# Decode layer with adaLN, sliding-window attention and a GEGLU FFN: K and V loaded in pairs of tiles, all of K ahead of V, with fewer loads and a shorter list of filler matmuls

## The chip, the cores and the metric

The kernel runs on one core of one Trainium2 chip. The metric is the device time of one execution in microseconds (us). The core has a matrix engine (TensorE, PE in the profile; its weight loads are PEld), a vector engine (VectorE, DVE), a scalar engine (ScalarE, ACT), GpSimd (POOL) and SyncE (SP), which here issues the DMA transfers. Engines run side by side, each through its own list of instructions in order, and wait for one another by semaphores.

## What is computed

One decode step for two sequences (B = 2, one token each, D = 640): modulation vectors from `c`, a norm, attention of 32 heads of 192 over the last W = 1024 rows of the caches, an output projection, a second norm and a GEGLU FFN with F = 1536. All in bf16.

```python
mod = (silu(c) @ w_mod).reshape(B, 6, 1, -1)        # sa, ca, ga, sb, cb, gb
h = layernorm(x) * (1 + ca) + sa
q = (h @ wq).reshape(B, 1, 32, 192).transpose(0, 2, 1, 3)
k = k_cache[:, :, Sk - W:, :];  v = v_cache[:, :, Sk - W:, :]
p = softmax(einsum('bhqd,bhkd->bhqk', q, k) * 192 ** -0.5)
o = einsum('bhqk,bhkd->bhqd', p, v)
x = x + ga * (o.transpose(0, 2, 1, 3).reshape(B, 1, 32 * 192) @ wo)
h = layernorm(x) * (1 + cb) + sb
return x + gb * ((gelu(h @ w_gate) * (h @ w_up)) @ w_down)
```

## The kernel before

**Layout.** A partition holds one quarter of a head's window: 32 heads times 4 quarters are the 128 partitions, and each has KP = 256 rows of 192 values of K and as many of V, per sequence. These 256 rows are cut in NTL = 4 tiles of J = 64 rows, 24576 bytes per partition. So there are 8 tiles of K and 8 of V over the two sequences.

**The ring and the order of loads.** Tiles go through a ring of NS = 5 slots, `ring` (L178). `items` (L322 to L325) fixes their order: the four K tiles of sequence 0, then V of sequence 0 and K of sequence 1 in turns, then V of sequence 1. `declare_ring` (L332) issues, on SP, the load of the next tile as soon as the code has declared the use of the tile that held its slot; at run time SP then waits (at L93) until the last reader of that slot is done. SP's list in order: w_mod, wq in two loads, K tiles, the interleaved tiles, the four loads of wo (L585, into `r1`, where wq was), then w_gate, w_up in two and w_down in three loads (L589 to L601, into slots 1 and 2), and the store of the result (L663). Each is one instruction at L260.

**Stages.** w_mod's matmuls (L391) and the first norm give hT; q is two groups of matmuls as wq lands (L414); `qsel` (L433) spreads q to the partitions as `qbc`.

*K loop.* It works on half tiles. `d_mul` (L454) multiplies 32 rows of K with q on DVE, in place. `p_reduce` (L465) adds up twelve slices of 16 values each on TensorE, with the identity as weights, in a bank of PSUM, and `d_rows` (L474) adds up the remaining 16 values on DVE. `filler` puts ND = 4 matmuls whose result nobody reads (`warm`, L444) ahead of each `p_reduce`.

*Softmax* (L478 to L498) is done once per sequence: a maximum per head, by way of a transpose and a broadcast matmul, the exponential on ACT, and the sum.

*PV.* `d_mask` (L502) spreads the exponentials of a tile over the 32 heads on DVE, in one of two buffers `Em`; `p_pv` (L514) multiplies with V in 32 matmuls of 384 columns, two side by side, summed over all tiles in bank BK_O. PV of sequence 0 lies between the K steps of sequence 1; PV of sequence 1 stands alone, with eight fillers after each tile but the last.

*Rest.* `normalize` (L528 and L532), `p_sel` (L540) for both sequences, four copies to `oc`, three transposes to `oT` (L578), the wo matmuls (L609) in four groups, `x1`, the second norm (L355 to L378), gate and up (L628) with gelu on ACT, the product (L642), a transpose, the down matmuls (L651) in three groups, two vector steps (L659, L661) and the store. `warm` is called between these steps with the counts in WO_WARM and WD_WARM and those written at the calls. An `nc.Block` (L665) closes the program, with an exchange of events between all engines at its end.

**Waits.** `_track` (L42) derives the waits from names of buffers: a reader waits for the last writer, a writer for all readers; banks of PSUM count as written by whoever reads them.

Of the kernel before, what the change touches and what calls it, by code (L numbers as in the profile page):

```python
# [5 lines left out]
ALU = mybir.AluOpType  # L6
ACTF = mybir.ActivationFunctionType
AX = mybir.AxisListType
# [95 lines left out]
def bass_adaLN_cond__sliding_block_cached__geglu_ffn__decode_kernel(  # L104
# [34 lines left out]
    NTL = KP // J  # L139
    JH = J // 2  # L140
    NQ = H * Dh
# [4 lines left out]
    NQC = RN // QC  # L146
    SCALE = float(Dh) ** -0.5
# [6 lines left out]
    NS = 5  # L154
    SL = J * Dh
    WQ_SPLIT = [3, 2]
    assert sum(WQ_SPLIT) == KT
    WO_SPLIT = [16, 16, 12, 4]
    OT_SPLIT = [16, 16, 16]
    assert sum(WO_SPLIT) == NT and sum(OT_SPLIT) == NT  # L160
    WU_SPLIT = [3, 2]
    assert sum(WU_SPLIT) == KT
    WD_SPLIT = [6, 4, 2]
    assert sum(WD_SPLIT) == FT
    ND = 4

    WO_WARM = [2, 15, 2, 10]
    WD_WARM = [7, 2, 0]

    es = ExitStack()  # L170
    with es:
# [6 lines left out]
        ring = sb("ring", [P, NS, J, Dh], BF16)  # L178
        ring_f = ring[:, :, :, :].rearrange("p s j d -> p (s j d)")
        def slot_f(slot, a, n):  # L180
            assert a + n <= SL
            return ring_f[:, slot * SL + a:slot * SL + a + n]


        assert KT * 6 * D <= 2 * SL and 2 * KT * F + FT * D <= 2 * SL
        wm_f = ring_f[:, 2 * SL:2 * SL + KT * 6 * D]
        wm_v = wm_f.rearrange("p (k n) -> p k n", k=KT)
        Qsel = slot_f(4, 0, 2 * HM * P).rearrange("p (b m n) -> p b m n", b=2, m=HM)
        qC = slot_f(4, 2 * HM * P, RN)
        wg_v = ring_f[:, SL:SL + KT * F].rearrange("p (k n) -> p k n", k=KT)  # L190
        wu_v = ring_f[:, SL + KT * F:SL + 2 * KT * F].rearrange("p (k n) -> p k n", k=KT)
        wd_v = ring_f[:, SL + 2 * KT * F:SL + 2 * KT * F + FT * D].rearrange("p (f n) -> p f n", f=FT)
        oc = slot_f(4, 0, RN)
        oT = slot_f(4, RN, NT * SQ).rearrange("p (t m) -> p t m", m=SQ)
        aC = slot_f(3, 0, FN)
        aT = slot_f(3, FN, FT * SQ).rearrange("p (f m) -> p f m", m=SQ)
# [3 lines left out]
        one = sb("one", [1, 1], F32)  # L200
# [20 lines left out]
        Sg = sb("Sg", [P, max(KP, FN)], F32)  # L221
        S_sb = Sg[:, 0:KP]
        gl = Sg[:, 0:FN]
        ones_f = Sg[:, 0:P]
        M1 = sb("M1", [P, 1], F32)
        gm = sb("gm", [1, H], F32)
        gx = sb("gx", [1, H, QP], F32)
        nb = sb("nb", [P, 1], F32)
        E_sb = sb("E_sb", [P, KP], BF16)
# [7 lines left out]
        BK_O = 3  # L237
# [13 lines left out]
        sem_wq = [S.sem("d_wq%d" % i) for i in range(len(WQ_SPLIT))]  # L251
        sem_wo = [S.sem("d_wo%d" % i) for i in range(len(WO_SPLIT))]
        sem_wg = S.sem("d_wg")
        sem_wu = [S.sem("d_wu%d" % i) for i in range(len(WU_SPLIT))]
        sem_wd = [S.sem("d_wd%d" % i) for i in range(len(WD_SPLIT))]
        sem_ring = [S.sem("d_ring%d" % i) for i in range(NS)]
# [9 lines left out]
        def dram_rows(v):  # L266
# [7 lines left out]
        S.op("pool", lambda e: e.memset(one[:, :], 1.0), writes=["one"], name="one")  # L274
        S.op("pool", lambda e: e.memset(ones_f, 1.0), writes=[("S", 0, 0), ("S", 0, 1), ("S", 1, 0), ("S", 1, 1)], name="ones_f")
        S.op("pool", lambda e: e.affine_select(out=ident_f[:, :], in_=ones_f, pattern=[[-1, P]],
                                                compare_op=ALU.is_equal, fill=0.0, base=0, channel_multiplier=1),
             reads=[("S", 0, 0), ("S", 0, 1), ("S", 1, 0), ("S", 1, 1)], writes=["ident_f"], name="ident_f")
# [3 lines left out]
        S.op("pool", lambda e: e.memset(Qsel, 0.0), writes=[("ring", 4, 0)], name="Qsel0")  # L282
# [18 lines left out]
        for b in range(2):  # L301
            for m in range(HM):
                S.op("dve", (lambda b, m: lambda e: e.tensor_copy(
                    out=Qsel[:, b, m, :].rearrange("p (a m t) -> p a m t", a=NJ, m=HM)[:, :, m, :],
                    in_=ident_f[:, BS * b:P:SQ].unsqueeze(2).broadcast_to([P, NJ, QP])))(b, m),
                    reads=["ident_f"], writes=[("ring", 4, 0)], name="Qsel%d%d" % (b, m))

        def half_key(slot, hf):
            return ("ring", slot, hf)

        def ring_keys(slot):
            return [half_key(slot, 0), half_key(slot, 1)]

        keep = {}
        S.dma("sp", k_dma(wm_f, w_mod.rearrange("(p k) n -> p (k n)", k=KT)), sem_wm, writes=ring_keys(2) + ring_keys(3), name="ld_wm")
        wq_src = A_wq.rearrange("(p k) n -> p k n", k=KT)
        wq_of = [(sum(WQ_SPLIT[:i]), sum(WQ_SPLIT[:i + 1])) for i in range(len(WQ_SPLIT))]
        keep["wq_dma"] = [S.dma("sp", k_dma(wq_v[:, ka:kb, :].rearrange("p k n -> p (k n)"), wq_src[:, ka:kb, :].rearrange("p k n -> p (k n)")),
                                sem_wq[i], writes=[("wq", i)], name="ld_wq%d" % i) for i, (ka, kb) in enumerate(wq_of)]


        items = [("k", 0, t) for t in range(NTL)]  # L322
        for t in range(NTL):
            items += [("v", 0, t), ("k", 1, t)]
        items += [("v", 1, t) for t in range(NTL)]  # L325
        place = {it: n for n, it in enumerate(items)}
        ring_state = {"next": 0, "done": set()}

        def slot_of(*it):
            return place[it] % NS  # L330

        def declare_ring(*consumed, upto=len(items)):  # L332
            ring_state["done"].update(place[it] for it in consumed)
            while ring_state["next"] < upto and (ring_state["next"] < NS or (ring_state["next"] - NS) in ring_state["done"]):
                n = ring_state["next"]
                kind, b, t = items[n]
                slot = n % NS
                cache = A_v_cache if kind == "v" else A_k_cache
                S.dma("sp", k_dma(ring[:, slot, :, :].rearrange("p j d -> p (j d)"),
                                  cache[b, :, K0:Sk, :].rearrange("h (q r) d -> h q r d", q=QP)[:, :, J * t:J * (t + 1), :].rearrange("h q r d -> h q (r d)")),  # L340
                      sem_ring[slot], writes=ring_keys(slot), name="ld_%s%d_%d" % (kind, b, t))
                ring_state["next"] += 1

        declare_ring(upto=2)


# [37 lines left out]
        def mod_part(part):  # L384
# [10 lines left out]
            S.op("pe", f, reads=["scT"] + ring_keys(2) + ring_keys(3), writes=[bank(bk)], name="mod%d" % part)  # L395
# [9 lines left out]
        declare_ring(upto=4)  # L405


        for i, (ka, kb) in enumerate(wq_of):
            def f(e, ka=ka, kb=kb):
                last = None  # L410
                for k in range(ka, kb):
                    for c in range(NQC):
                        for j in range(NJ):
                            last = e.matmul(ps[SQ * j:SQ * j + SQ, BK_H + c, 0:QC], lhsT=hT[:, k, :],  # L414
                                            rhs=wq_v[:, k, RN * j + QC * c:RN * j + QC * (c + 1)],
                                            start=(k == 0), stop=(k == KT - 1), tile_position=(0, SQ * j), skip_group_check=True)
                return last
            keep["q"] = S.op("pe", f, reads=["hT", ("wq", i)], writes=[bank(BK_H + c) for c in range(NQC)], name="q%d" % i)

# [29 lines left out]
        def filler(n=1):  # L449
            warm(n * ND, BK_W)  # L450

# [264 lines left out]
```

## Time and profile before

| | |
|---|---|
| median of three runs | 189.1 us (189.08, 189.10, 189.87) |
| profiled execution: span from first to last instruction | 187.5 us |
| PE busy | 131.9 us, 1068 matmuls |
| DVE busy | 107.1 us, 114 instructions |
| ACT, POOL busy | 13.9 us, 4.9 us |
| HBM read | 76.88 MB, 410 GB/s over the span |
| loads of K, of V | 8 and 8, 3072 KB each |
| readerless matmuls (L444) | 174, 34.6 us |
| chain that ended last, by engine | DMA 53%, PE 21%, DVE 20% |

The median lies 1.6 us above the span of the profiled execution; the sums below are made against the span. A row of the profile names the line of the kernel, the engine, the operation, out<-in, the number of instructions and the busy time. The page's shares are averages over the whole span, so that each stage has to be looked at by itself, in the timeline and in windows. The granted clock is the share of its full speed that TensorE was allowed. The chain of waits is followed back from the last instruction, at each step to what released it.

### The profile page before, as it was taken

To read this page: it belongs to the slowest core of one execution; us is meant where nothing else is said; L and a number is where in the kernel's file an instruction comes from. 1 tells how busy PE (TensorE), PEld (TensorE's weight loads), DVE (VectorE), ACT (ScalarE), POOL (GpSimd) and SP (SyncE) were. 2 spreads that over 40 slices of the span, in tenths; PEclk is the share of its full clock that TensorE was granted. 3 is DMA by queue.
4 is the path that set the end of the run, shared out by engine and by line. 5 is a ranking of instruction groups with operands and counts; after the bars stand their busy time and mean duration, and the time that the engine had idled before them with its cause. 6 is when DMAs were issued, how large, how long until landed. Compare 5 with 4: busy or idle time off the path is not lost.

```text
span 187.5 us, 2388 instructions
## 1 busy us (share of the span) xinstructions
PE 131.9 (70%) x1068; PEld 65.3 (35%) x1068; DVE 107.1 (57%) x114; ACT 13.9 (7%) x24; POOL 4.9 (3%) x12
## 2 busy tenths in 40 slices
PE   0004543565999989449999939929539998859993
PEld 0001221251443333125454514504225656535441
DVE  6811400029599998389599398298475602903431
ACT  2003200031000000000000000000010002300400
POOL 8100000000000000000000000000000000000000
PEclk9999999555699999966999996987957999999999
DMA  7999899999999999999999999999999999999980
GB/s 262 394 457 440 385 454 412 425 451 440 435 425 421 419 418 440 451 430 430 425 419 412 430 456 435 428 419 425 419 435 446 427 424 424 421 412 420 414 345 5
DMA packets 4221, 77.02 MB, mean 411 GB/s; under 512 B 500, under 2 KB 500, under 8 KB 1140
## 3 DMA queue, kind: packets, MB, share of 16 engines
q1 hardware_dynamic: 4188, 76.88, 96.3%
q8 instruction: 8, 0.13, 0.3%
q10 hardware_dynamic: 24, 0.01, 0.0%
q14 instruction: 1, 0.01, 0.0%
HBM read 76.88 MB, written 0.00 MB: 410 GB/s over the span
## 4 chain that ended last, share of the span: by engine, by line
DMA 53%; PE 21%; DVE 20%; issue 2%; SPq 2%; ACT 0%; DVEq 0%
DMA ring<-in_A_k_cache_dram 31%; DMA r<-in_A_wo_dram 22%; DVE ring L454 14%; PE ps L465 8%; PE ps L444 5%; PE ps L514 4%; DVE Sg L474 2%; SPq L260 2%; PE ps L609 1%; DVE Em L502 1%; PE ps L628 1%; PE ps L651 1%; DVE ring L348 0%; ACT E_sb L493 0%; DVE ring L642 0%
## 5 line engine op out<-in xcount | busy, mean ns | idle before, releaser
L454 DVE TENSOR_TENSOR ring<-ring,qbc 128x6144 bf16<-128x6144 bf16 x16 | 53.5, 3352 | 10.6 <-DMA ring<-in_A_k_cache_dram 10.6
L465 PE MATMUL ps<-ring,ident_b 128*128 128x512 bf16 x192 | 50.0, 416 | 10.9 <-DVE ring L454 10.8
L444 PE MATMUL ps<-qbc,ident_b 128*128 128x384 bf16 x174 | 34.6, 333 | 2.9 <-issue 2.2
L465 PEld LDWEIGHTS ps<-ring,ident_b 128*128 128x128 bf16 x192 | 19.2, 104 | 38.5 <-DVE ring L454 15.0
L514 PE MATMUL ps<-ring,Em 128*64 128x384 bf16 x256 | 26.3, 367 | 4.9 <-DVE Em L502 4.9
L444 PEld LDWEIGHTS ps<-qbc,ident_b 128*128 128x128 bf16 x174 | 15.9, 100 | 18.5 <-issue 8.4
L514 PEld LDWEIGHTS ps<-ring,Em 128*64 128x64 bf16 x256 | 15.4, 122 | 15.0 <-DVE Em L502 6.4
L502 DVE TENSOR_TENSOR Em<-E_sb,M32b 128x2048 bf16<-128x2048 bf16 x8 | 18.2, 2283 | 4.0 <-PE ps L514 4.0
L474 DVE TENSOR_REDUCE Sg<-ps 128x32 f32<-128x512 f32 x16 | 11.0, 687 | 9.1 <-PE ps L465 9.1
L391 PE MATMUL ps<-ring,scT 128*32 128x480 bf16 x40 | 4.4, 601 | 14.9 <-DMA ring<-in_w_mod_dram 14.9
L414 PE MATMUL ps<-r,hT 128*32 128x384 bf16 x80 | 6.8, 523 | 8.8 <-DMA r<-in_A_wq_dram 8.8
L424 DVE CAST ring<-ps 128x384 bf16<-128x384 f32 x4 | 2.0, 553 | 15.7 <-PE ps L414 14.7
L414 PEld LDWEIGHTS ps<-r,hT 128*32 128x32 bf16 x80 | 3.1, 140 | 12.7 <-issue 6.0
L391 PEld LDWEIGHTS ps<-ring,scT 128*32 128x32 bf16 x40 | 1.3, 133 | 16.3 <-issue 16.3
L528 ACT ACTIVATE On<-ps,rden 32x192 bf16<-32x192 f32 x4 | 1.6, 412 | 71.1 <-PE ps L514 61.3
L532 DVE TENSOR_SCALAR On<-ps,rden 32x192 bf16<-32x192 f32 x4 | 1.7, 418 | 7.4 <-ACT On L528 7.4
L616 DVE TENSOR_TENSOR lnt<-ps,modC 128x160 f32<-128x160 f32 x1 | 0.3, 324 | 7.3 <-PE ps L609 7.3
L609 PE MATMUL ps<-r,ring 128*32 128x160 bf16 x192 | 4.1, 233 | 0.5 <-DVE ring L578 0.5
L578 DVE STREAM_TRANSPOSE ring<-ring 128x512 bf16<-128x512 bf16 x3 | 4.1, 1423 | 0.1
L493 ACT ACTIVATE E_sb<-Sg,nb 128x256 bf16<-128x256 f32 x2 | 1.0, 507 | 40.8 <-DVE nb L492 40.8
L609 PEld LDWEIGHTS ps<-r,ring 128*32 128x32 bf16 x192 | 3.3, 96 | 1.9 <-issue 1.5
L433 PE MATMUL ps<-ring 128*128 128x192 bf16 x16 | 2.7, 361 | 1.2 <-DVE ring L424 1.2
(68 smaller groups left out, 54.7 us busy)
## 6 DMA issues: line engine op xcount, KB each, us to landing
ring<-in_A_k_cache_dram SPq DMA_DIRECT2D x8, 3072.0 KB, 29.6
ring<-in_A_v_cache_dram SPq DMA_DIRECT2D x8, 3072.0 KB, 25.1
r<-in_A_wo_dram SPq DMA_DIRECT2D x2, 2560.0 KB, 37.9
ring<-in_w_mod_dram SPq DMA_DIRECT2D x1, 4800.0 KB, 14.0
r<-in_A_wq_dram SPq DMA_DIRECT2D x1, 4608.0 KB, 24.5
r<-in_A_wq_dram SPq DMA_DIRECT2D x1, 3072.0 KB, 32.6
r<-in_A_wo_dram SPq DMA_DIRECT2D x1, 1920.0 KB, 44.5
ring<-in_B_w_gate_dram SPq DMA_DIRECT2D x1, 1920.0 KB, 18.0
```

Source lines behind the costliest of these rows:

```text
L260: return lambda e: e.dma_start(dst, src)
L391: last = e.matmul(ps[SQ * j:SQ * j + SQ, bk, 0:3 * DN].rearrange("p (i n) -> p i n", i=3), lhsT=scT[:, k, :], rhs=wm_v[:, k, 3 * part * D: ...
L414: last = e.matmul(ps[SQ * j:SQ * j + SQ, BK_H + c, 0:QC], lhsT=hT[:, k, :], rhs=wq_v[:, k, RN * j + QC * c:RN * j + QC * (c + 1)], start=( ...
L433: last = e.matmul(ps[:, BK_O, b * Dh:(b + 1) * Dh], lhsT=Qsel[:, b, m, :], rhs=qC[:, m * Dh:(m + 1) * Dh], start=(m == 0), stop=(m == HM - ...
L444: last = e.matmul(ps[:, bk, 0:2 * Dh], lhsT=ident_b[:, :], rhs=qbc[:, :, :].rearrange("p b d -> p (b d)"), start=True, stop=True)
L454: S.op("dve", lambda e: e.tensor_tensor(out=ring[:, ks, hf * JH:(hf + 1) * JH, :], in0=ring[:, ks, hf * JH:(hf + 1) * JH, :], in1=qbc[:, b ...
L465: last = e.matmul(o_ap, lhsT=ident_b[:, :], rhs=ring[:, ks, hf * JH:(hf + 1) * JH, ci * GC:(ci + 1) * GC], start=(ci == 0), stop=(ci == NC ...
L474: S.op("dve", lambda e: e.tensor_reduce(out=S_sb[:, a:a + JH], in_=ps[:, hf, 0:JH * GC].rearrange("p (j c) -> p j c", j=JH), axis=AX.X, op ...
L502: S.op("dve", lambda e: e.tensor_tensor(out=Em[:, t % 2, :, :], in0=E_sb[:, J * t:J * (t + 1)].unsqueeze(2).broadcast_to([P, J, H]), in1=M ...
L514: last = e.matmul(ps[r:r + 2 * H, BK_O, 0:ON], lhsT=Em[:, t % 2, 2 * jp:2 * jp + 2, :].rearrange("p j c -> p (j c)"), rhs=ring[:, vs, 2 * ...
L578: S.op("dve", (lambda t0, nt: lambda e: e.transpose(oT[:, t0:t0 + nt, :], oc.rearrange("p (q k) -> p k q", k=NT)[:, t0:t0 + nt, :]))(t0, n ...
L609: last = e.matmul(ps[SQ * j:SQ * j + SQ, BK_M, 0:DN], lhsT=oT[:, t, :], rhs=wo_v[:, t, DN * j:DN * j + DN], start=(t == 0), stop=(t == NT ...
```

## The change

K and V tiles are loaded in pairs (PJ = 128 rows, 49152 bytes per partition; 8 loads). There are three places for pairs, two in `pp` and the third in `r1`, which first holds wq and later wo. The order is all of K, then all of V. K is worked off in quarters of a pair (`q` from 0 to 3, 32 rows as before). Both sequences share one softmax, after the last K. PV of both sequences follows, each summed in its own bank. wq, w_up are one load each, wo and w_down two. q's matmuls have 512 columns. `held` is a matmul that leaves the weights of the one before in place; a sum over twelve slices and a group of fillers load the identity once. Fillers are left only in the K loop, four per quarter. The Block is gone.

```diff
-    NS = 5
-    SL = J * Dh
-    WQ_SPLIT = [3, 2]
-    WO_SPLIT = [16, 16, 12, 4]
+    NP = 3
+    SL = PJ * Dh
+    WO_SPLIT = [32, 16]
     OT_SPLIT = [16, 16, 16]
-    WU_SPLIT = [3, 2]
-    WD_SPLIT = [6, 4, 2]
-    ND = 4
-    WO_WARM = [2, 15, 2, 10]
-    WD_WARM = [7, 2, 0]
+    WD_SPLIT = [10, 2]
+    NF = 4
...
+        pp = sb("pp", [P, 2, PJ, Dh], BF16)
+        places = [pp[:, 0, :, :], pp[:, 1, :, :], r1[:, 0:SL].rearrange("p (j d) -> p j d", j=PJ)]
...
-        items = [("k", 0, t) for t in range(NTL)]
-        for t in range(NTL):
-            items += [("v", 0, t), ("k", 1, t)]
-        items += [("v", 1, t) for t in range(NTL)]
...
+        S.dma("sp", k_dma(wq_v.rearrange("p k n -> p (k n)"), A_wq.rearrange("(p k) n -> p (k n)", k=KT)),
+              sem_wq, writes=place_keys(2) + ["wq"], name="ld_wq")
+        items = [(kind, b, t) for kind in ("k", "v") for b in range(2) for t in range(NPR)]
+        place_of = {it: k for it, k in zip(items, (0, 1, 2, 0, 1, 2, 0, 1))}
+        def load_next():
+            it = items[state["next"]]
+            state["next"] += 1
+            kind, b, t = it
+            k = place_of[it]
+            cache = A_v_cache if kind == "v" else A_k_cache
+            S.dma("sp", k_dma(places[k].rearrange("p j d -> p (j d)"),
+                              cache[b, :, K0:Sk, :].rearrange("h (q r) d -> h q r d", q=QP)[:, :, PJ * t:PJ * (t + 1), :].rearrange("h q r d -> h q (r d)")),
+                  sem_pl[k], writes=place_keys(k), name="ld_%s%d_%d" % (kind, b, t))
+        load_next()
...
         mod_part(1)
-        declare_ring(upto=4)
+        load_next()
...
+            for k in range(KT):
+                for c in range(NQW):
+                    for j in range(NJ):
+                        last = e.matmul(ps[SQ * j:SQ * j + SQ, BK_H + c, 0:QW], lhsT=hT[:, k, :],
...
+        load_next()
...
+        def held(e, out, lhsT, rhs, start, stop):
+            i = mybir.InstMatmult(name=nc.get_next_instruction_name(), engine=mybir.EngineType.PE,
+                                  ins=[e.lower_ap(rhs), e.lower_ap(lhsT)], outs=[e.lower_ap(out)],
+                                  start_tensor_calc=start, stop_tensor_calc=stop, tile_size=(P, P), tile_position=(0, 0), ldweights=False)
+            return e.add_instruction(i)
...
                 for ci in range(NCH):
-                    last = e.matmul(o_ap, lhsT=ident_b[:, :], rhs=ring[:, ks, hf * JH:(hf + 1) * JH, ci * GC:(ci + 1) * GC],
-                                    start=(ci == 0), stop=(ci == NCH - 1))
+                    put = e.matmul if ci == 0 else lambda *a, **k: held(e, *a, **k)
+                    last = put(o_ap, lhsT=ident_b[:, :], rhs=places[k][:, JH * q:JH * (q + 1), ci * GC:(ci + 1) * GC],
+                               start=(ci == 0), stop=(ci == NCH - 1))
...
-        steps = [(b, t, hf) for b in range(2) for t in range(NTL) for hf in range(2)]
+        steps = [(b, t, q) for b in range(2) for t in range(NPR) for q in range(NH)]
+        for n, (b, t, q) in enumerate(steps):
+            d_mul(b, t, q)
+            warm(NF, BK_W)
+            p_reduce(b, t, q)
+            if n > 0:
                 d_rows(*steps[n - 1])
+            if q == NH - 1 and state["next"] < 6:
+                load_next()
         d_rows(*steps[-1])
-        softmax(1)
-        for t in range(NTL):
-            d_mask(1, t)
-            p_pv(1, t)
-            if t < NTL - 1:
-                filler(2)
-            else:
-                p_sel(0)
-        normalize(1)
-        warm(4, 1)
+        softmax()
+        d_mask(0, 0)
+        d_rden()
+        for b in range(2):
+            for t in range(NTL):
+                if b or t:
+                    d_mask(b, t)
+                p_pv(b, t)
+                if t % 2 == 1 and state["next"] < len(items):
+                    load_next()
+                if b == 1 and t == 2:
+                    p_sel(0)
+            normalize(b)
         p_sel(1)
-        warm(14, 1)
...
-                  sem_wo[i], writes=[("wo", i)], deps=keep["wq_dma"] + [keep["q"]], name="ld_wo%d" % i)
+                  sem_wo[i], writes=[("wo", i)], deps=[keep["pv", 0, NTL - 1]], name="ld_wo%d" % i)
...
-        r3_dead = [keep["red", 1, NTL - 1], keep["pv"]]
+        dead = [keep["pv", 1, NTL // 2 - 1]]
...
-        with nc.Block() as block:
...
+        S.emit("sp", nc.sync)
+        nc.sync.wait_ge(sem_out, 16)
+        S.emit("act", nc.scalar)
+        S.emit("pool", nc.gpsimd)
+        S.emit("dve", nc.vector)
+        S.emit("pe", nc.tensor)
```

The joint `softmax` takes the maxima and sums of both sequences in two columns (a 128x512 maximum in place of 128x256, one transpose, one broadcast, one sum matmul, two exponentials). The two w_up loads become one; q's copies are three of 512 columns in place of four of 384. `Qsel`, `qC`, `oc`, `oT`, `aC` and `aT` have memory of their own now, in place of parts of the ring.

## The prediction

> **What bounds the kernel now.** I read the page's DMA rows first, then the DMA queues in three windows, the chain of waits, and the timeline with the granted clock.
>
> ```profile
> span 187.5 us, 2388 instructions
> ...
> q1 hardware_dynamic: 4188, 76.88, 96.3%
> ```
>
> Sixteen DMA engines are busy for 96.3% of the span with 76.88 MB that the change doesn't reduce (same tensors, each once). The queue windows (16 to 24 us, 60 to 100, 175 to 180; packets, MB, share of 16 engines):
>
> ```profile
> q1 hardware_dynamic: 96, 3.54, 102.3%
> ...
> q1 hardware_dynamic: 795, 17.18, 100.3%
> ...
> q1 hardware_dynamic: 339, 2.09, 100.9%
> ```
>
> The share is 100% while rows of 36864, of 24576 and of some 6850 bytes flow: there is no gap to close, and what is left is the cost per row and what follows the last landing. Per row: 102.3% of 16 x 8.0 us over 96 rows is 1364 ns; 100.3% of 16 x 40 us over 699 rows (17.18 MB / 24576) is 918 ns; 100.9% of 16 x 5 us over 305 rows (339 packets less 34 under 512 B) is 265 ns. The first and third give 36.6 ns per 1000 bytes and 14 ns per row besides; the first and second give 26 ns.
>
> The chain of waits at its end (start, us, what):
>
> ```profile
> 123.12 40.39 DMA r<-in_A_wo_dram
> ...
> 163.55 1.29 PE ps L609 x64
> 164.84 1.24 PE ps L444 x7
> 166.08 2.21 issue
> 168.30 1.48 PE ps L444 x8
> ...
> 182.27 1.24 PE ps L444 x7
> 183.52 0.39 PE ps L651 x16
> ```
>
> From 163.5 on the end hangs on TensorE: wo's matmuls, the second norm, the FFN, with readerless matmuls (L444) between them, and 2.21 us in which TensorE got no instruction. The last weights land at about 183.5 (third w_down issue 158.5, 25.0 us to landing). So DMA and this tail end within a microsecond of each other: both must get shorter for a gain.
>
> The clock (stretch, PE busy, granted clock is the column before the last two):
>
> ```profile
> 77.78:81.19 3.41, 1.03 (x5) 0.67 (x5) 1.45 (x5) 0.60 (x2) 0.00 (x0) 1.00 0.94 404
> 81.19:84.60 3.41, 1.79 (x12) 1.08 (x14) 3.41 (x2) 0.00 (x0) 0.00 (x0) 0.50 1.06 454
> 84.60:88.02 3.42, 3.42 (x24) 1.62 (x18) 3.42 (x2) 0.00 (x0) 0.00 (x0) 0.50 1.04 446
> 132.39:135.80 3.41, 1.48 (x7) 0.57 (x5) 1.65 (x5) 0.00 (x0) 0.00 (x0) 1.00 1.03 440
> 139.22:142.63 3.41, 2.99 (x20) 1.73 (x22) 2.56 (x2) 0.00 (x0) 0.00 (x0) 0.50 1.01 432
> 166.52:169.94 3.42, 1.64 (x24) 0.94 (x28) 0.00 (x0) 0.00 (x0) 0.00 (x0) 1.00 1.02 425
> 169.94:173.35 3.41, 3.41 (x78) 1.99 (x67) 1.46 (x4) 0.00 (x0) 0.00 (x0) 1.00 1.00 418
> ```
>
> The clock changes only at the edges of 3.41 us windows: down to 0.50 after a window with 1.48 us of matmul or less, up after one with 2.99 or more; 1.64 kept it. At 0.50 a PV tile costs twice:
>
> ```profile
> 82.81 5.33 PE L514 MATMUL ps<-ring,Em 128*64 128x384 bf16 x32 [2.45 <-DVE Em L502]
> 149.34 2.79 PE L514 MATMUL ps<-ring,Em 128*64 128x384 bf16 x32
> ```
>
> **The change, part by part.**
>
> *Longer rows.* K/V: 16 loads become 8, so each engine handles 8 x 8 = 64 rows fewer. wq in one load saves 8, wo two of four 16, w_up 8, w_down 8: 104 in all, 72 of them by the last V. At 14 ns: 1.0 us by the last V, 1.5 at the end; at 26 ns 1.9 and 2.7. I take 14, from the wider spread of sizes; the lower end is nothing. A loss I exclude: the longest rows in the trace run fastest (442 GB/s in 16 to 24 us, 430 in 60 to 100). Fewer issues of 0.54 us on SP lie beside the full queue.
>
> *Does the queue stay full?* A place is refilled only when a whole pair is used up, so I follow SP's waits in its order. By bytes at 0.43 MB/us and the landings seen now, pair (0,0) lands near 48.4 (19.07 MB ahead of and in it) and qbc is ready near 45: wq lands at 34.3, q has 60 matmuls of 512 columns, four side by side: 15 x 0.427 at half clock = 6.4; then 1.1 of copies, 2.7 of qsel and 0.5, rows as now. That late start is therefore the load's. A quarter costs DVE 3.27 + 0.60 = 3.87 us, as between 58.3 and 76 now; the first two wait 2 us for a slow TensorE, as at 48 to 50 now. So quarter 3 is summed at 67.9, 7 at 83, 11 at 99, 15 at 114.3. Queued data end, at those points, at about 76, 91, 105 and 120: 6 to 9 us in hand each time. The joint softmax (6.1 us from rows to mask now, 0.5 more for twice the row) starts PV at 120.4, PV(0,1) ends near 129 and frees the last place while V (1,0) still runs to 135: 6 in hand. wo waits for PV(0,3) (134), the FFN weights for PV(1,1) (144 to 147, since DVE normalizes batch 0, 1.9 us, ahead of the mask of (1,0)); the queue then holds data to 150 and 168. So no bubble, at a price of nothing; gone, each microsecond over the 6 is one at the end.
>
> *One load of the identity per sum, four warm matmuls per quarter.* The trace has no matmul without a weight load; its bounds are 2.76/12 = 0.23 us, as now, and half of the slow 0.44. Either way 12 + 4 take at most 3.57 of DVE's 3.87: nothing, hidden by DVE's multiply. At the lower one (0.22 and, for a filler, half of the slow 0.36) TensorE still works 3.36 of 3.87 us, 87%, far over the 1.64/3.42 that kept the clock.
>
> *The tail.* The last V pair lands whole: 151.4 for the last V tile now (121.4 issued, 30 to landing, from the two tiles' 27.7 median), less 1.0: 150.4. TensorE has then been idle for 3 us or more, so it starts at half clock and steps up u after its start, at the end of the first full window, u from 3.0 to 6.8. Two PV tiles are 32 rounds of 0.32 (0.16 at full clock) and sel0 1.28 (0.64): 0.5u + 6.0 us. At u = 5, PV ends at 158.9 (156.3 now). Then as now 1.9 normalize, 0.85 sel1, 1.16 copies, and two transposes, 2.8, as the first wo piece is 32 tiles: wo starts at 165.6 (161.8 now), both idle gaps having dropped the clock again. For sel1 after its pause of 1.9 I keep the full clock, since the pause would have to fall into one window to leave 1.49 us of work there, the amount that lost the clock at 132.39; lost, sel1 takes 1.5, and 0.65 is added. [...] wo is 48 rounds of 0.133 (0.067): 0.5u + 3.4 = 5.9: 171.5, after its landing (169.5 - 1.2). Now it ends at 171.5 too: the 19 fillers between and the 2.21 us without instructions pay for the later start. Norm 4.6, plus 0.2 for a slow statistic: 176.3. Gate and up back to back at half clock 5 x 0.32 x 2 + 0.2 = 3.4 (3.9 now, with ten fillers): 179.75. To the down matmuls 1.61, as now: 181.4; the first ten tiles of w_down land at 182.8 - 1.5 = 181.3. Down at half clock 1.33 + 0.2, then 0.27: 183.2 (184.6 now). The two vector steps 0.74, store and wait 1.72, as now: 185.7.
>
> *No Block.* Now the engines' closing events run from SP's branch at 187.1 to 187.5; without them 0.4 us goes, which the 185.7 already holds. Its bounds are 0 and 0.4.
>
> **Sum**: 187.5 to 185.7, less 1.8 in the profiled execution: last V 1.0 earlier, PV 3.6 longer behind it, wo to hT 2.4 regained, FFN with the down step 1.6, closing 0.4. The median is 1.6 above the span (189.1 to 187.5) and I keep that: 187.3 us, 1.0% faster.
>
> **The rivals.**
>
> *Same: the tail's clock steps up late, or instructions run out.* u = 6.8 in PV adds 0.9 and no step in wo 0.9: 187.5, so 189.1. One more stall like the 2.21: 187.9, so 189.5. For it: the stall fell in the same stretch; against: at half clock wo uses instructions half as fast, and TensorE has 484 fewer in all (176 + 268 of the identity's loads and fillers, 40 of q). [...] Chance 0.18.
>
> *Same: the long rows are cut up and nothing is saved in DMA.* All landings stay: last V 151.4, w_down 1.5 later, and the tail ends at 187.0: 188.6. Against: rows of 36864 and 38400 show no cut. 0.07.
>
> *Slower: the clock stays at 0.50 from the last V on.* PV and sel0 11.7, sel1 1.5, wo 6.6, the rest as above: 190.2, so 191.8. For it: the fillers of the tail are gone, and every pause there is over 1.9 us. Against: each full window in the trace was followed by 1.00, and PV fills one. It decides once the tail loses 2.7 us against the sum. 0.10.
>
> *Slower: the queue runs dry.* If TensorE falls to half clock in the K loop, a quarter takes 12 x 0.427 + 4 x 0.32 = 6.4; four such quarters cost 10 us, 4 beyond the 6 in hand: 189.7, so 191.3. Against: a TensorE that is the bound is wholly busy and steps up. 0.10.
>
> **How the numbers follow.** Forecast 0.55. A run can tell 0.5% from no change, that is 188.15 to 190.05: faster 0.55, same 0.18 + 0.07 = 0.25, slower 0.20. The lower end is 26 ns per row with a quick clock, where the last landing (183.5 - 2.7 = 180.8) plus 0.9 of down and 2.5 of closing bounds it: 184.2, or 185.8. The upper end takes in the same-cases, 189.5. The forecast's own range is 185.8 to 188.1.
>
> **What would show it.** Right: DMA share 100% through 168 us, PV of the last pair from 150.4 at clock 0.50, wo ending near 171.5, fewer packets by about 1900, no L444 after PV, the last landing near 182. Wrong: a DMA dip between 60 and 135, K quarters over 3.9 us, an idle "issue" on TensorE after 150, or last landings at 183.5.

## The result and the profile after

| | before | after |
|---|---|---|
| median | 189.72 us (188.98 to 190.34) | 188.67 us (186.79 to 189.11) |
| ratio, 95% interval | | 0.9942 [0.9921, 0.9963] |
| profiled execution: time, span | span 187.5 | 187.92, 186.7 |
| spans | 187.0 to 188.8 (53 executions beside the experiments) | 185.5 to 187.8, ten of 15 between 187.3 and 187.8 |
| time less span | 1.7 to 1.8 (the same 53) | 1.2 to 1.3 |

The kernel became faster by 0.6%, with an interval of 0.4 to 0.8%. The forecast was 1.0%, 187.3 us. The three runs shown ahead of the prediction were at the low end of what the kernel before does: over 15 runs its median is 0.6 us higher.

The page of the kernel after, from the top: span and instructions; the DMA queues with packets, MB and share; the bytes read; and the group of the wo matmuls, with busy time and mean ns of one, then the idle time of TensorE ahead of them and what ended most of it.

```profile
span 186.7 us, 1853 instructions
...
q1 hardware_dynamic: 2316, 76.88, 95.9%
q8 instruction: 6, 0.10, 0.2%
...
HBM read 76.88 MB, written 0.00 MB: 412 GB/s over the span
...
L586 PE MATMUL ps<-r,oT 128*32 128x160 bf16 x192 | 5.0, 276 | 6.8 <-DVE oT L559 4.1
```

The same 76.88 MB come in 2316 packets where there were 4188, at 412 GB/s where there were 410. The last row is the one to stop at: ahead of the wo matmuls TensorE was idle for 6.8 us, and the transposes of `oT` explain 4.1 of them. The other 2.7 us are in the chain that ended last (start, us, what), from the last V pair on:

```profile
119.64 7.46 PE ps L500 x64
...
127.16 23.33 DMA pp<-in_A_v_cache_dram
...
150.62 4.71 PE ps L500 x32
155.33 0.77 PE ps L525 x8
156.10 2.74 PE ps L500 x32
...
165.61 4.73 PE ps L586 x172
170.34 2.74 issue
173.08 0.26 PE ps L586 x2
...
178.12 3.42 PE ps L602 x39
...
183.13 1.04 PE ps L620 x47
184.20 0.34 DVE lnt L626
```

After 190 of the 192 wo matmuls TensorE waits 2.74 us for nothing that the chain names ("issue"), and only then runs the last two. This is the sign that the prediction itself gave of being wrong, an idle "issue" on TensorE after 150. All that follows is late by the wait. The loads are not at fault: w_down had landed at 182.5, before its matmuls began at 183.1.

Stretches of the clock's windows in the tail of the kernel after (from and to; length; busy time of PE, PEld, DVE, ACT and POOL; granted clock; DMA share; GB/s):

```profile
151.28:154.69 3.41, 3.41 (x26) 2.28 (x24) 0.00 (x0) 0.00 (x0) 0.00 (x0) 0.52 1.19 509
154.69:158.11 3.42, 3.42 (x42) 2.33 (x40) 0.00 (x0) 0.00 (x0) 0.00 (x0) 1.00 0.93 395
158.11:161.52 3.41, 1.54 (x18) 0.84 (x14) 0.83 (x2) 0.82 (x2) 0.00 (x0) 1.00 0.89 384
161.52:164.93 3.41, 0.00 (x0) 0.00 (x0) 3.28 (x4) 2.15 (x3) 0.00 (x0) 0.98 0.94 402
164.93:168.35 3.42, 2.74 (x88) 2.77 (x92) 1.86 (x2) 0.00 (x0) 0.00 (x0) 0.52 1.05 449
168.35:171.76 3.41, 1.99 (x114) 1.79 (x103) 0.00 (x0) 0.00 (x0) 0.00 (x0) 1.00 1.00 419
```

PV of the last pair starts at half clock and is at full clock one window later, as the prediction had it. wo starts slow too, but the next window is granted 1.00. A mean of 0.52 over 3.42 us is 3.28 us at 0.50 and 0.14 us at 1.00, so these stretches end 0.14 us after the clock's change. The trace has it at 168.21: the clock is 0.50 in 164.80 to 168.21, in which TensorE had 2.60 us of work, and 1.00 in the 3.41 us after. So wo was at half clock for some 2.6 us, not for 5, and its work took 5.0 us where the sum had 5.9.

### The profile page after: what moved, and what is told of

The parts are those of the page before. It is cut to its first block, busy times and chain, and to the rows that moved or that the text cites. A ratio compares the mean times of both kernels' runs of the same rounds, so it can differ in the third digit from the quotient of the medians.

```text
span 186.7 us, 1853 instructions
## 1 busy us (share of the span) xinstructions
PE 108.8 (58%) x933; PEld 35.0 (19%) x709; DVE 105.5 (57%) x108; ACT 14.0 (7%) x24; POOL 4.8 (3%) x11
## 3 DMA queue, kind: packets, MB, share of 16 engines
q1 hardware_dynamic: 2316, 76.88, 95.9%
HBM read 76.88 MB, written 0.00 MB: 412 GB/s over the span
## 4 chain that ended last, share of the span: by engine, by line
DVE 39%; DMA 38%; PE 18%; issue 2%; ACT 1%; SPq 0%; DVEq 0%
DMA pp<-in_A_k_cache_dram 25%; DVE pp L434 19%; DMA pp<-in_A_v_cache_dram 12%; PE ps L500 8%; DVE r L434 7%; DVE Sg L454 5%; PE ps L420 3%; PE ps L586 3%; PE ps L602 2%; DVE oT L559 1%; DVE Em L485 1%; PE ps L525 1%; PE ps L620 1%; DVE oc L401 1%; PE ps L447 1%
## 5 line engine op out<-in xcount | busy, mean ns | idle before, releaser
L434 DVE TENSOR_TENSOR pp<-pp,qbc 128x6144 bf16<-128x6144 bf16 x12 | 40.1, 3346 | 8.8 <-DMA pp<-in_A_k_cache_dram 8.8
L420 PE MATMUL ps<-pp,ident_b 128*128 128x512 bf16 x132 | 32.0, 393 | 0.0
L500 PE MATMUL ps<-pp,Em 128*64 128x384 bf16 x192 | 22.0, 402 | 12.5 <-DMA pp<-in_A_v_cache_dram 7.0
L500 PEld LDWEIGHTS ps<-pp,Em 128*64 128x64 bf16 x192 | 13.5, 136 | 20.5 <-issue 7.5
L434 DVE TENSOR_TENSOR r<-r,qbc 128x6144 bf16<-128x6144 bf16 x4 | 13.4, 3343 | 0.0
L390 PE MATMUL ps<-r,hT 128*32 128x512 bf16 x60 | 6.1, 591 | 11.5 <-DMA r<-in_A_wq_dram 11.5
L447 PE MATMUL ps<-pp,ident_b 128*128 128x512 bf16 x12 | 4.9, 407 | 13.0 <-DVE pp L434 13.0
L420 PE MATMUL ps<-qbc,ident_b 128*128 128x384 bf16 x48 | 10.4, 326 | 0.0
L420 PE MATMUL ps<-r,ident_b 128*128 128x512 bf16 x44 | 10.2, 379 | 0.0
L427 PEld LDWEIGHTS ps<-qbc,ident_b 128*128 128x128 bf16 x16 | 1.6, 98 | 37.1 <-issue 37.1
L427 PE MATMUL ps<-qbc,ident_b 128*128 128x384 bf16 x16 | 5.2, 326 | 0.7 <-ACT qbc L399 0.7
L500 PE MATMUL ps<-r,Em 128*64 128x384 bf16 x64 | 5.4, 327 | 0.0
```

Of the source, the lines that this page charges most:

```text
L390: last = e.matmul(ps[SQ * j:SQ * j + SQ, BK_H + c, 0:QW], lhsT=hT[:, k, :], rhs=wq_v[:, k, RN * j + QW * c:RN * j + QW * (c + 1)], start=( ...
L420: return e.add_instruction(i)
L427: last = put(ps[:, bk, 0:2 * Dh], lhsT=ident_b[:, :], rhs=qbc[:, :, :].rearrange("p b d -> p (b d)"), start=True, stop=True)
L434: S.op("dve", lambda e: e.tensor_tensor(out=places[k][:, JH * q:JH * (q + 1), :], in0=places[k][:, JH * q:JH * (q + 1), :], in1=qbc[:, b, ...
L447: last = put(o_ap, lhsT=ident_b[:, :], rhs=places[k][:, JH * q:JH * (q + 1), ci * GC:(ci + 1) * GC], start=(ci == 0), stop=(ci == NCH - 1))
L500: last = e.matmul(ps[r:r + 2 * H, BK_O[b], 0:ON], lhsT=Em[:, t % 2, 2 * jp:2 * jp + 2, :].rearrange("p j c -> p (j c)"), rhs=places[k][:, ...
```

## The experiments

Medians are in us, ratios are to the kernel before in runs on the same chip. There were three chips: one for e0 to e3, one for e4 to e7 and one for e8 to e11. The medians of the kernel before were 189.74, 189.43 and 189.63 there, so a difference of medians across these groups is uncertain by some 0.3 us.

| run | edit to the kernel after | median (range) | ratio, 95% interval | span of the profiled run |
|---|---|---|---|---|
| e0_after | none | 188.36 (186.83 to 189.43) | 0.9929 [0.9899, 0.9959] | 185.6 |
| e1_nf3 | three fillers per quarter | 187.48 (187.35 to 187.72) | 0.9886 [0.9856, 0.9917] | 186.2 |
| e2_nf5 | five fillers per quarter | 188.51 (187.08 to 189.07) | 0.9914 [0.9882, 0.9945] | 186.8 |
| e3_rows24k | each pair as two loads | 188.24 (187.36 to 190.04) | 0.9937 [0.9906, 0.9968] | 187.1 |
| e4_block | Block back | 189.39 (188.04 to 190.36) | 0.9989 [0.9960, 1.0019] | 187.7 |
| e5_reload | identity loaded for each matmul | 187.59 (187.52 to 187.67) | 0.9890 [0.9868, 0.9912] | 186.2 |
| e6_wd642 | three fillers, w_down in 6/4/2 | 187.17 (186.95 to 187.25) | 0.9864 [0.9842, 0.9887] | 186.0 |
| e7_lastv | three fillers, last V pair in two loads | 187.72 (186.99 to 188.06) | 0.9890 [0.9869, 0.9912] | 185.7 |
| e8_best | e7, e9 and 16 fillers in the tail | 187.07 (186.93 to 187.35) | 0.9869 [0.9841, 0.9897] | 185.9 |
| e9_splits | three fillers, w_down in 6/4/2, w_up in 3/2 | 186.98 (186.86 to 187.08) | 0.9863 [0.9835, 0.9890] | 185.6 |
| e10_block_nf3 | three fillers, Block back | 188.35 (187.49 to 188.48) | 0.9928 [0.9903, 0.9953] | 186.7 |
| e11_wo8 | wo in six loads of 10240-byte rows | 187.95 (187.77 to 188.23) | 0.9916 [0.9884, 0.9948] | 186.6 |

### Where does TensorE stop: e0_after, e1_nf3, e2_nf5

If TensorE runs out of instructions at a fixed place of its list, the stop must move when instructions ahead of it are added or taken out. If it waits for data or a semaphore, it stays. A filler in the K loop is one instruction and there are 16 quarters (1853 instructions on the page of after, 1837 on that of e1_nf3); a wo matmul is two instructions, a weight load and a matmul (192 of each in after). So one filler more per quarter must move the stop 16 instructions, 8 wo matmuls, ahead; one less moves it 8 matmuls later, past the end of wo.

```diff
-    NF = 4
+    NF = 3
```

That is e1_nf3; e2_nf5 has `NF = 5`.

> The changed kernel again, as the base of the runs beside it. Its first profile had a gap of 2.74 us in TensorE's wo matmuls with nothing to wait for (after the 190th of 192). Theory A: TensorE runs out of instructions at a fixed place of its list, so the gap comes again after the same matmul. Theory B: the gap has to do with the weights or with what DMA does just then; it moves or is missing from execution to execution. Ratio to the kernel before 0.992 to 0.996 in either case.

> Three readerless matmuls per K quarter in place of four: 16 instructions fewer on TensorE ahead of wo, nothing else. Theory A: the place where instructions run out moves 16 instructions on, past wo's last matmul and into the idle time of the second norm; wo ends near 170.6 instead of 173.3, the down matmuls then start when w_down lands (about 181.7 to 182.4 instead of 183.1), and the span is 185.3 to 186.1, 0.6 to 1.4 us less than the changed kernel's. Theory B: the gap stays in wo and the span stays within 0.5 us of the changed kernel's. Both: K quarters stay at 3.87 us.

> Five readerless matmuls per K quarter: 16 instructions more on TensorE. Theory A: the gap stays in wo but comes 16 instructions, that is 8 matmuls, earlier (after about the 182nd), costs the same 2.7 us, and the span is that of the changed kernel within 0.5 us. Theory B: the same place as in the changed kernel, or none. K quarters stay at 3.87 us, as TensorE has 12 x 0.21 + 5 x 0.16 = 3.4 us of work in each.

The wo matmuls in the timelines (start, us, engine, line, operation, count, and in brackets the idle time before): of e0_after,

```profile
164.94 6.10 PE L586 MATMUL ps<-r,oT 128*32 128x160 bf16 x190 [4.10 <-DVE oT L559]
171.97 0.25 PE L586 MATMUL ps<-r,oT 128*32 128x160 bf16 x2 [0.92 <-issue]
```

of e1_nf3,

```profile
166.31 5.12 PE L586 MATMUL ps<-r,oT 128*32 128x160 bf16 x192 [4.10 <-DVE oT L559]
```

and of e2_nf5:

```profile
165.86 4.71 PE L586 MATMUL ps<-r,oT 128*32 128x160 bf16 x182 [4.09 <-DVE oT L559]
172.51 0.38 PE L586 MATMUL ps<-r,oT 128*32 128x160 bf16 x10 [1.94 <-issue]
```

The stop stays at 190 in the unchanged kernel, moves by exactly 8 matmuls to 182 with 16 instructions more, and is gone with 16 fewer. This settles the place: it is a count in TensorE's list, not an event of another engine. The length isn't fixed: 0.92 us where wo ran slowly (6.10 us), 2.74 where it ran faster (4.73). Work and wait together are 7.0 and 7.5 us. So a faster wo did not end earlier, it only waited longer.

The page of after has 6 packets and 0.10 MB on the queue marked "instruction", 16384 bytes each in the trace; the page of before has 8 packets and 0.13 MB. Two packets fewer for 494 matmuls and weight loads fewer (2136 to 1642) is an estimate of some 250 instructions in one. The stop in wo costs 0.9 to 2.7 us.

The trace also has the time of each packet. The queues of the kernel after in 165.61 to 170.5, from wo's first matmul on, and in 170.5 to 171.8, in the stop:

```profile
q1 hardware_dynamic: 144, 2.09, 100.2%
...
q1 hardware_dynamic: 48, 0.58, 108.0%
q8 instruction: 1, 0.02, 5.1%
```

The packet runs from 170.63 to 171.69, and TensorE goes on at 173.08. In all six profiles with the wait (after, e0_after, e2_nf5, e3_rows24k, e4_block, e11_wo8) TensorE goes on 1.3 to 1.6 us after the end of such a packet. In all six the stop comes after the 1473rd record of TensorE in the trace (matmuls, weight loads and events). The stall of 2.21 us in the kernel before is of the same kind: its packet runs from 165.74 to 166.80, TensorE goes on at 168.29, and the stop comes after record 1729, which is 1473 + 256. So the two places lie 256 records apart, in line with some 250 instructions in a packet, and the times fit a wait of TensorE for its next block of 256 instructions. The 14 packets of before and after fit it too: counted in steps of 256 from these places (193 to 1985 in before, 193 to 1473 in after) there is one packet to each place, and 12 of them start 0.8 to 5.7 us after TensorE has gone past it, two 0.7 and 3.8 us ahead.

With the wait gone, the median falls by 0.9 us against e0_after (1.2 against the first runs of the kernel after), and the runs lie within 0.4 us where they spread over 2.6. The packet still comes, from 171.57 to 172.61, but wo has ended at 171.43 and the place now lies behind it. The end now hangs on another thing, in the chain of e1_nf3:

```profile
146.27 35.46 DMA pp<-in_B_w_down_dram
...
181.87 1.82 PE ps L620 x42
...
183.71 0.34 DVE lnt L626
```

The down matmuls wait for the first ten tiles of w_down, and run at half clock (PEclk on the page of e1_nf3 is 5 tenths in the last two slices, from 176.9 on; 1.82 us against 1.04 in after).

### Does the load of the identity matter: e5_reload

```diff
-                    put = e.matmul if i == 0 else lambda *a, **k: held(e, *a, **k)
+                    put = e.matmul
...
-                    put = e.matmul if ci == 0 else lambda *a, **k: held(e, *a, **k)
+                    put = e.matmul
```

> The identity is loaded for every matmul again, 4 readerless matmuls per quarter as in the changed kernel: 14 x 16 = 224 instructions more on TensorE ahead of wo. Theory A, now more exact: instructions come in pieces of 256; the next piece is asked for when one is begun and takes some 5 us to come (from the place 256 instructions ahead of the gap to its end: 4.8 to 5.4 us in four profiles), so TensorE starves where it uses up 256 within less, as in wo. With 224 more the ends of pieces move to 158 instructions (79 matmuls) into wo, whose piece was asked for during PV and has come, and to 414, past wo's 384: no gap in wo, wo ends at 170 to 171.5, and the span is 0.6 to 1.4 us less than the changed kernel's, as with three readerless matmuls. Theory B (the number of instructions is what counts): 224 more make more gaps, span the same or longer. Both: K quarters stay at 3.87 us, so that loading the identity once has no worth of its own in the K loop.

This adds 224 weight loads ahead of wo and leaves NF at 4. The group of wo matmuls in e5_reload:

```profile
L586 PE MATMUL ps<-r,oT 128*32 128x160 bf16 x192 | 4.9, 281 | 4.1 <-DVE oT L559 4.1
```

All idle time is that of `oT` again, and the kernel is 0.8 us faster than e0_after at 187.59 (0.7 by the ratios). More instructions made it faster, since the place moved by 224 to about the 78th matmul of wo; a block that ends there begins, by this count, ahead of wo, before the pauses of the copies and transposes. That the next one has that time to come is the author's estimate; the trace shows that its packet ran from 154.5 to 155.6, ten microseconds ahead of wo's first matmul at 165.96, and no other came before wo's end. The quarters of the K loop stayed at DVE's 3.27 + 0.60 us. So holding the identity is worth nothing of its own here, as the prediction had it; what it did was to shift the place from about the 78th matmul of wo to the 190th.

### Are the long rows worth what was said: e3_rows24k

```diff
-            S.dma("sp", k_dma(places[k].rearrange("p j d -> p (j d)"),
...
+            for h in range(2):
+                a = J * h
+                parts.append(S.dma("sp", k_dma(places[k][:, a:a + J, :].rearrange("p j d -> p (j d)"),
...
-                 reads=["qbc"], writes=[("pl", k, q)], name="mul%d_%d_%d" % (b, t, q))
+                 reads=["qbc"], writes=[("pl", k, q)], deps=loaded["k", b, t], name="mul%d_%d_%d" % (b, t, q))
```

> Each pair is loaded as two transfers with rows of 24576 bytes, one after the other, and every user still waits for both: the row length and the number of transfers alone. By the prediction's 14 ns per row (64 rows per engine) the last V lands 0.9 us later, at about 151.4 instead of 150.5, w_down 0.9 us later, and the span grows by 0.5 to 0.9 us. Rival: the row length is worth nothing, landings and span stay within 0.3 us. TensorE's list is the same, so the gap in wo comes as in the changed kernel.

Rows of 24576 bytes again; the users still wait for a whole pair. From the chain of e3_rows24k:

```profile
151.35 4.65 PE ps L513 x32
...
166.28 6.34 PE ps L599 x143
172.62 0.98 issue
173.61 0.26 PE ps L599 x2
```

PV of the last pair starts at 151.35 where it was 150.62 and, in e0_after, 150.51. That is 0.73 to 0.84 us for 64 rows more on each DMA engine, 11 to 13 ns per row, a little less than the 14 ns of the prediction. Only the K and V rows were tried. In the total it can't be seen (188.24 against 188.36), which fits the wait in wo standing behind it; no run has the shorter rows without that wait.

### What is the Block worth: e4_block, e10_block_nf3

```diff
-        S.emit("sp", nc.sync)
-        nc.sync.wait_ge(sem_out, 16)
...
+        with nc.Block() as block:
...
```

> The changed kernel with the Block of the kernel before put back, nothing else. By the prediction the engines' closing events come again after the store has landed: 0.4 us from SP's branch to the last event, where the changed kernel ends with SP's wait; the span grows by 0.4 us. Rival: the changed kernel closes with the same exchange in another way and nothing is gained, 0.0 us. The Block also adds a branch ahead of TensorE's list; if that shifts the place where instructions run out, it does so by one instruction, and the gap stays within two matmuls of where it was.

> The Block put back where the gap in wo is absent (three readerless matmuls per quarter), so that its price shows without the scatter of the gap. The run with the Block in the changed kernel had 1.7 us between span and time, the ones without it 1.2 to 1.3, and a closing longer by 0.4 us. If both belong to the Block, the span is 186.5 to 186.7 and the time 0.7 to 0.9 us over that of the run with three readerless matmuls (187.5), that is 188.2 to 188.4. Rival: only the closing belongs to it, 0.4 us, 187.9.

With the Block back, and all the rest of the change in, the time is that of the kernel before: 0.9989 [0.9960, 1.0019]. So in the kernel as changed, the Block's removal is all of the gain that can be measured. With the Block in and the wait gone (e10_block_nf3) the ratio is 0.9928: the rest of the change does gain, and in e4_block the wait in wo takes it back. Where the wait is gone, the Block costs 0.87 us (188.35 against 187.48), which is two things. Within the span it is the events of the closing exchange; the last of them in e10_block_nf3 (line, engine, duration in ns, start):

```profile
L632 PEldq EVENT_SEMAPHORE  x1: 51/51/51, 186.7 to 186.7; - x1
```

The medians of the spans are 186.6 and 186.2, so 0.4 us. The other 0.5 us lie outside the span: time less span is 1.7 to 1.8 us with the Block, 1.2 to 1.3 without it, in every execution of these kernels. What runs there no profile shows. The pair also repeats e1's finding with the Block in: 189.39 with the wait in wo, 188.35 without, 1.04 us.

### Why does the wait in wo take so long: e11_wo8

That the length of wo's rows has a part in how long TensorE waits was the author's estimate, which no run had shown. If it does, shorter rows during wo should shorten the time from the place 256 instructions earlier to the end of the stop.

```diff
-    WO_SPLIT = [32, 16]
+    WO_SPLIT = [8, 8, 8, 8, 8, 8]
```

> The changed kernel with wo in six loads of 8 tiles (rows of 10240 bytes in place of 40960 and 20480). Theory A: the gap in wo stays at its place (within a few matmuls, since each load adds a wait). [...]

The timeline of e11_wo8:

```profile
164.73 5.54 PE L586 MATMUL ps<-r,oT 128*32 128x160 bf16 x190 [2.77 <-DVE oT L559]
172.19 0.25 PE L586 MATMUL ps<-r,oT 128*32 128x160 bf16 x2 [1.92 <-issue]
```

The stop is at the same place. One block of 256 instructions, 128 matmuls, ahead of it is the 62nd matmul of wo, which TensorE passed at 166.7; the last two ran 5.5 us later. By the same count it is 4.9 to 5.5 us in after, e0, e2, e3 and e4. That the next block is asked for at that place is inferred; the trace shows only when its packet ran. In e5_reload a packet starts at 154.51, 1.1 us before TensorE reaches the place one block ahead of the one that it serves (record 1217, 155.61), so the request can come earlier than this count has it. So the 5.5 us of e11_wo8 are no shorter than the 4.9 to 5.5 us with the longer rows.

But ahead of the packet the rows are the same in both kernels. The queue in 169 to 170.5 of after and in 168.7 to 169.7 of e11_wo8, just ahead of the packets at 170.63 and 169.74:

```profile
q1 hardware_dynamic: 40, 0.61, 96.1%
...
q1 hardware_dynamic: 28, 0.43, 101.0%
```

Both are rows of 15360 bytes, those of the FFN's weights. The last row of wo had ended at 168.3 (168.7 in e11_wo8), and the last of the 40960-byte rows of after at 162.2, before its wo matmuls began. So the edit changes little of what lay ahead of the packet, and the run does not decide whether the length of the rows there has a part. Of the 5 us, the packet itself takes 1.0 to 1.1 and the time from its end to the next matmul 1.3 to 1.6; what holds it up before it starts is open.

wo's first group needs fewer transposes (idle 2.77 for 4.10), but the median is not told apart from that of e0_after: 0.9916 [0.9884, 0.9948] against 0.9929 [0.9899, 0.9959].

### What binds next: e6_wd642, e7_lastv, e8_best, e9_splits

With three fillers the end hangs on the last landings. Four kernels go at that, all with `NF = 3`.

In e6_wd642, e8_best and e9_splits:

```diff
-    WD_SPLIT = [10, 2]
+    WD_SPLIT = [6, 4, 2]
```

In e8_best and e9_splits, w_up in two loads, each with its own semaphore:

```diff
+    WU_SPLIT = [3, 2]
...
-        ffn_gu(BK_G[1], wu_v, "wu", "wu", 0, KT)
+        for i, (ka, kb) in enumerate(wu_of):
+            ffn_gu(BK_G[1], wu_v, ("wu", i), "wu%d" % i, ka, kb)
```

In e7_lastv and e8_best, the last V pair in two loads, and PV of each of its tiles waits for one of them:

```diff
+            for h in range(2):
+                a = J * h
+                S.dma("sp", k_dma(places[k][:, a:a + J, :].rearrange("p j d -> p (j d)"),
...
```

In e8_best alone, readerless matmuls after wo, after the second norm's statistic and after w_up:

```diff
+        warm(4, 1)
         S.op("dve", lambda e: e.tensor_tensor(out=lnt[:, 0, :], in0=ps[:, BK_M, 0:DN], in1=modC[:, 2, :], op=ALU.mult),
...
         layer_norm("ln2", 1, 3)
+        warm(8, 1)
...
+        warm(4, 1)
         S.op("dve", lambda e: e.tensor_tensor(out=aC[:, :], in0=ps[:, BK_G[1], 0:FN], in1=gl, op=ALU.mult),
```

> Three readerless matmuls per quarter (no gap), and w_down in three loads of 6, 4 and 2 tiles in place of 10 and 2. With three readerless matmuls the end hung on the load of 10 tiles (waited for until 181.8) and the 48 down matmuls behind it at half clock, 1.8 us. Now 24 of them can run ahead, and behind the last landing (about 182.3) there are 8: the down matmuls end near 182.6 to 182.9 instead of 183.7, span 185.1 to 185.5, about 1 us less than with three readerless matmuls alone. Rival: the chain through norm and FFN is as late as the load (down starts at 181.4 to 181.9 by it) and the gain is under 0.4 us.

> Three readerless matmuls per quarter, and the last V pair in two loads, whose first half's user doesn't wait for the second half. PV of that half starts some 7 us earlier (near 143.5 instead of 150.5) and the second half's from 150.5 on, so that PV ends 2.5 to 4 us earlier. If the end hangs on the last landings (the reading of the run with three readerless matmuls), the span stays within 0.3 us of that run. Rival: the end still hangs on TensorE's chain from the last V on, as the prediction's sum had it, and the span falls by 1 us or more.

> Put together: three readerless matmuls per quarter, the last V pair and w_up in two loads each, w_down in three (6, 4, 2), and readerless matmuls only in the pauses of the tail (4 behind wo, 8 behind the norm's statistic, 4 behind gate and up) so that TensorE is at full clock in the down matmuls. If the end hangs on the last landing (about 182.3) with 8 down matmuls, two vector steps and the store behind it, the span is 184.8 to 185.3 and the ratio to the kernel before 0.979 to 0.985. Rival: the chain from the landing of w_up (178.3 in the run with three w_down loads) still sets the end, 185.6 to 186.0.

> The same without the early last V and without the readerless matmuls in the tail: three per quarter, w_up in two loads, w_down in three. Behind the second part of w_up (about 178.2) stand 8 matmuls instead of 20, and TensorE is at half clock: down starts near 181.2 and ends near 183.0, span 185.4 to 185.7. If the full clock in the tail is worth what its rounds say (12 rounds of down at 0.133 or 0.067, 0.8 us), this run is 0.4 to 0.8 us behind the one with readerless matmuls; if not, they are equal.

e6_wd642 gave 0.3 us by the medians, no more than the chips differ, and not the full microsecond that the wait in front of the down matmuls seemed to hold. Its chain has the next landing:

```profile
144.25 33.98 DMA pp<-in_B_w_up_dram
...
178.28 1.82 PE ps L602 x19
...
181.69 1.82 PE ps L620 x37
```

w_up lands at 178.2 and gates the FFN. Splitting it too gives e9_splits, whose end waits for the last piece of w_down alone:

```profile
148.07 34.52 DMA pp<-in_B_w_down_dram
...
182.64 0.49 PE ps L625 x6
...
183.15 0.34 DVE lnt L631
```

e7_lastv starts PV of the last pair earlier and gains nothing in time (187.72 against 187.48): TensorE only reaches the next landings sooner. Its wo matmuls now wait for their own load, 6.55 us before the first group and 2.26 before the second. e8_best missed its expectation, with a span of 185.9 for 184.8 to 185.3. It adds e7's split and the tail fillers to e9; the last landing came at 182.9 (182.6 in e9), and 187.07 is no better than e9's 186.98. So the two edits together are worth nothing once landings bind; the fillers of the tail were not tried alone. e9_splits is the fastest version found, not told apart from e6 and e8 by its interval: 1.4% below the kernel before, and 1.2 us (by the ratios) to 1.4 us (by the medians) below e0_after, with one filler fewer in each quarter and two loads more.

## What the prediction had right, and the step that failed

**Right, by the profile after.** The first K pair landed at 48.6 (forecast 48.4). The queue never went dry: between 20 and 160 the data queue's share is 99.8%. Quarters take 3.87 us. PV begins at 119.6 (120.4), the last V pair lands at 150.5 (150.4), PV and sel0 end at 158.8 (158.9), wo starts at 165.6 (165.6). Gate and up take 3.42 us (3.4). The clock came up in the second window of PV, at 154.56, and held through sel1, at 1.00 to 164.80. From the last V pair to wo's first matmul the sum is right to 0.1 us, in part by luck: the clock rose 3.9 us into PV where the sum had 5, which is 0.5 us less, and small terms (0.1 us before PV, some 0.3 in it, 0.1 behind it) made up for it.

**The step that failed** is the one in the tail: "wo is 48 rounds of 0.133 (0.067): 0.5u + 3.4 = 5.9: 171.5 … the 19 fillers between and the 2.21 us without instructions pay for the later start". It takes a stall that the trace of before shows out of the sum, and puts none in. wo ended at 173.3: its work was 0.9 shorter (the clock rose after 2.6 us), the wait for instructions 2.7 longer. The rival named it ("One more stall like the 2.21", in a case with a chance of 0.18) and held against it that "at half clock wo uses instructions half as fast, and TensorE has 484 fewer in all". Both were the wrong measure. Fewer instructions do not remove a place where they run out, they move it, as e1, e2 and e5 show in steps of 16 and 224; and wo uses them fast: 384 instructions, 192 matmuls and their loads, in some 5 us. The 4.9 to 5.5 us from the place one block ahead to the end of the stop were not hidden in wo; with the place moved behind wo (e1) or to the 78th matmul (e5) there was no stop. The stall of before is the same wait one block further on (record 1729 for 1473), so it was no chance event of that kernel that a shorter list would take away.

**Mis-sized terms, which partly cancel.** (a) "No Block … Its bounds are 0 and 0.4" and "The median is 1.6 above the span … and I keep that": the removal gives 0.4 in the span and 0.5 outside it, and the second half was left out. (b) The down step: forecast 181.4 to 183.2 at half clock. In after it started late, at 183.1, and ran in 1.04 us at full clock (1.00 in 181.87 to 185.28), which gave back 0.7 of the 1.7 us lost. (c) The last landing: 1.5 us earlier was forecast, 182.5 against 183.5 is 1.0; in e1 the matmuls waited for w_down until 181.8. With the wait in wo taken out (e1), the span is 186.2 where the sum had 185.7, and this landing is the difference: the down step begins at 181.87 for 181.4 and takes 1.82 us, as forecast.

**In sum**, for the profiled execution: wo's end +1.8, the down step -0.7, rounding and store -0.1 make the span 186.7 for 185.7; outside it 1.2 for 1.6 makes 187.9 for 187.3. Most executions are longer than the profiled one, with spans of 187.3 to 187.8; the profiles taken with spans of 186.8 and 187.1 (e2, e3) have the wait together with a down step at half clock or a late PV, but none was taken of the longest. The size of the gain was thus 0.6% for 1.0%, with the forecast's base 0.6 us low as well.

## What to carry to other kernels

When a timeline has a stall marked "issue" on an engine that uses many small instructions, try it as a fixed place in that engine's list before it is put down to noise: work out how many instructions the change adds or removes ahead of it, see where the place then falls, and move it with a few instructions. Here 16 more moved it from the 190th matmul of wo to the 182nd, and with 16 fewer or 224 more the stall was gone. The trace had a sign of it: in all seven profiles with the stall, before among them, a packet on the queue marked "instruction" ended 1.3 to 1.6 us before TensorE went on. Before costing a change to loads or matmuls, look for such a wait behind it on the same path: here the kernel without it was 0.9 us faster. And a saving at the very end can lie outside the span, as 0.5 us of the Block's 0.87 did, so compare time less span as well as spans.

## What the runs showed of the hardware

TensorE waited 0.9 to 2.7 us for instructions in wo, a stream of 384 small ones, and 224 instructions more made the kernel 0.8 us faster. It went on 1.3 to 1.6 us after an instruction packet of 16384 bytes had ended, and the stops of the kernels before and after lie 256 records apart. From its first matmul to its last, wo took 7.0 to 7.7 us in the six profiles with the wait, 4.8 to 6.2 in e1, e5, e6, e9 and e10, which haven't got it. In the traces of before and after the 26 recorded stretches at one granted clock, but for the last of each, are 3.41 us long or a multiple of it (up to 61.44). In after the clock rose at the end of a window of 3.41 us with 2.60 us of TensorE work (164.80 to 168.21), so it rose without a full window there. It did not rise after one with 2.54 us in e3_rows24k (165.41 to 168.82), where wo's matmuls took 6.34 us, nor after one with 2.68 us in e1_nf3 (176.54 to 179.95), so the amount of work alone does not decide it. Closing this program with a Block cost some 0.5 us that no profile shows (time less span 1.7 to 1.8 us with it, 1.2 to 1.3 without).
